# Later sums of squares in a first expert network's weight split and in the values' split, one high half a step, and sixteen squares on another engine

## The chip, the cores and the metric

The kernel runs on one core of one Trainium2 chip. The metric is the device time of one execution in microseconds, the median of several runs. Five engines of the core take part: TensorE (PE; its weight loads are PEld), VectorE (DVE), ScalarE (ACT), GpSimd (POOL) and SyncE (SP, which here only issues DMAs). Each engine takes its instructions in the order in which the program wrote them, and waits at the first whose inputs aren't ready.

## What is computed

```python
def _attn_ref(q, k, v, s):            # 4 batches, 8 heads, 576 positions, 64 wide
    scores = scale * np.matmul(q, k.transpose(0, 1, 3, 2))
    cum = np.cumsum(np.maximum(s, 0.0), axis=-1)
    bias = -(cum[:, :, :, None] - cum[:, :, None, :])
    scores = np.where(causal, -1000000000.0, scores + np.minimum(bias, 0.0))
    attn = np.exp(scores - np.max(scores, axis=-1, keepdims=True))
    return np.matmul(attn / (np.sum(attn, axis=-1, keepdims=True) + 1e-09), v)

def _moe_ref(x, w_in, w_out):         # 2304 tokens, 512 -> 2048 -> 512
    h = np.maximum(x @ w_in, 0.0)
    return h * h @ w_out

def _moe2_ref(x, w_in, w_out):
    h = x @ w_in
    return h * np.cos(h) @ w_out

x = attention output as (2304, 512); x = _moe_ref(x, ...); return _moe2_ref(x, ...)
```

## The kernel before, in words

Every matrix product is made of three products of half-precision or reduced parts (high by high, high by low, low by high; `PASSES`). A float32 operand is split for that: a high part is rounded on ScalarE, a low part is the difference, on VectorE.

The tokens go through attention and the first network in nine blocks of 256 (blocks 0 to 8). While attention works on block k + 1, the first network works on block k; block 8 has no attention beside it. Its hidden layer has 16 chunks of 128. For chunk f, `g1` (L1149) makes 12 products of 256 columns into one half of the PSUM tile `hps` (the halves alternate, L1161), `gact` (L1172) rectifies (L1177), squares (L1180) and rounds the high part `gh` (L1181), all on ScalarE, `grest` (L1184) makes the low part `gl` on VectorE (L1187), and `g2` (L1190), two chunks behind, makes 12 products into the output's PSUM.

The program is written step by step (`step`, L1326). A step holds one or two of these first and second products, a row of attention jobs, and the side work that falls due in it. Within a step each engine's queue gets, in this order: the exponentials, the first network's product, the weights' bit work and low halves (`w_step`, `w_lows`), then `gact`, then the weights' conversion of the first network (`c_step`), the scores, a second product, the transposes of attention's output (`turn`, which write the left part of the PSUM tile `xps`), the values' sums, the value products, and last `c_total`, and the values' late work.

Three pieces of side work are touched:

- The first network's first weights are used as float32 parts in blocks 0 to 2 and as float16 parts from block 3 (`KC`) on. `c_step` (L890) makes the latter in blocks 1 to 3: sixteen squares with row sums (`c_square`, L860, ScalarE), one sum over the partitions for the first `SQ_A` of them and one for the rest (`c_total`, L921, a small product into columns of `xps`), the scales from it (`c_scales`, L842, VectorE), and for each of 16 chunks an addition (`c_add`, L872, VectorE), a high half (`c_high`, L878, ScalarE) and a low half (`c_low`, L883, VectorE). The counter t is the chunk that comes next, counted from block 0.
- The values of attention are split in sixteen groups of two heads. A group has a load (`v_load`, L437, by GpSimd, into one buffer), a square with row sums (L447, ScalarE), a sum over the partitions (L453, TensorE, into `xps`), a scale (L462, VectorE), a high part (L476, ScalarE), a low part (L482, VectorE) and a store. `v_steps` sets the steps from due times, `v_add` writes the list.
- In block 8, where the second network's weights and the first network's output are prepared too: their bit work (L981, L985), clipping (L975) and squares (L1060), scales (L1076 to L1081), high halves (L1008) and low halves in pairs (L1051), and the splitting of y on GpSimd (L1241, L1253).

After block 8 the second network runs in five larger blocks of tokens (L1610, L1671, L1762).

## Time and profile before

| | us |
|---|---|
| median of 3 runs | 972.58 |
| lowest and highest | 971.02, 973.68 |
| the profiled execution | 972.91 |
| its span, first to last instruction | 970.8 |
| TensorE busy in it | 937.3 |
| VectorE, ScalarE busy | 769.7, 709.7 |

A row of a timeline gives start, duration, engine, line, operation, what is written and read, and in brackets how long the engine had been idle before it and what ended that. Several instructions of one kind stand in one row as x2 or x12. The durations of products overlap, as their ends are modelled; their starts are read. A wait that is put down to one instruction can be for several, of which that came last.

### The profile page before, as it was taken

Reading aid. Unit: us, or ns where it says so; the run is one execution under the profiler, and the core shown is the slowest. Engines: PE = TensorE matmul, PEld = TensorE weight load, DVE = VectorE, ACT = ScalarE, POOL = GpSimd, SP = SyncE. Lnnn points to the kernel's source line nnn. Section 1 sums busy time; section 2 is a strip of 40 time slices with the busy share of each in tenths; the row PEclk is TensorE's granted clock in tenths of the full one; section 3 lists DMA queues with packets and bytes.
Section 4 is the critical chain, followed back from the end, with each engine's and each line's share of the span. In section 5 each row is a group of like instructions: output and inputs, shape, how many; then the busy total and the mean of one; then the engine's idle time right before and its main releaser. Section 6 shows DMA issues by size and latency. Waiting matters only on the chain.

```text
span 970.8 us, 21039 instructions
## 1 busy us (share of the span) xinstructions
PE 937.3 (97%) x7474; PEld 726.9 (75%) x7474; DVE 769.7 (79%) x1944; ACT 709.7 (73%) x1625; POOL 159.9 (16%) x298
## 2 busy tenths in 40 slices
PE   6999999989999999999999999999999999999997
PEld 5899998988989988999989986445544456666664
DVE  6899986789798866787997375888788788798774
ACT  6799887878898767676776686677777666565553
POOL 2001123222211222222330022430000000001101
PEclk9999999999999999999999999999999999999999
DMA  8984799657998987589999679210000000112001
GB/s 246 312 271 149 168 213 227 168 145 151 200 183 191 204 195 170 134 177 174 211 215 158 217 267 362 66 44 23 1 1 1 22 1 22 49 60 67 23 22 66
DMA packets 158074, 135.38 MB, mean 139 GB/s; under 512 B 109272, under 2 KB 132128, under 8 KB 157968
## 3 DMA queue, kind: packets, MB, share of 16 engines
q1 hardware_dynamic: 147664, 123.78, 50.8%
q0 software_dynamic: 10304, 10.24, 5.2%
q8 instruction: 59, 0.97, 0.4%
q14 instruction: 47, 0.39, 0.1%
HBM read 93.91 MB, written 15.83 MB: 113 GB/s over the span
## 4 chain that ended last, share of the span: by engine, by line
PE 59%; DVE 6%; ACT 3%; issue 2%; DMA 2%; SPq 0%; DVEq 0%; ACTq 0%
PE o L1671 18%; PE hp L1610 12%; PE y L1197 11%; PE hps L1165 9%; PE bank L1762 5%; PE qkp L567 2%; PE pvs L697 2%; DVE k L415 1%; DVE sb L585 1%; DMA raw<-in_qk_dram 1%; DMA rw<-in_w_dram 1%; DMA vb<-v_d 1%; DVE wt L1678 1%; PE xps L752 0%; ACT sb L608 0%
## 5 line engine op out<-in xcount | busy, mean ns | idle before, releaser
L1197 PE MATMUL y<-gh,wt 128*128 128x256 f32 x1152 | 237.7, 289 | 0.0
L1197 PEld LDWEIGHTS y<-gh,wt 128*128 128x128 f32 x1152 | 188.6, 190 | 1.2
L1671 PE MATMUL o<-wt,gh 128*128 128x512 f16 x576 | 171.3, 379 | 1.5 <-ACT gh L1649 1.3
L1197 PE MATMUL y<-gl,wt 128*128 128x256 f32 x576 | 162.9, 283 | 0.5 <-DVE gl L1187 0.5
L1165 PE MATMUL hps<-xh,w 128*128 128x256 f16 x1152 | 142.0, 273 | 2.6 <-ACT g L1177 2.4
L1610 PE MATMUL hp<-yh,wt 128*128 128x512 f16 (+1 forms) x448 | 124.9, 348 | 0.0
L1165 PEld LDWEIGHTS <-w 128*128 128x128 f16 x1152 | 106.1, 98 | 17.8 <-issue 4.2
L1197 PEld LDWEIGHTS y<-gl,wt 128*128 128x128 f32 x576 | 109.9, 191 | 1.4 <-DVE gl L1187 0.9
L1671 PE MATMUL o<-wt,gl 128*128 128x512 f16 x288 | 109.2, 379 | 0.0
L1610 PEld LDWEIGHTS <-wt 128*128 128x128 f16 x672 | 63.9, 98 | 59.1
L1671 PEld LDWEIGHTS <-gh 128*128 128x128 f16 x576 | 56.3, 98 | 56.3 <-ACT gh L1649 1.6
L608 ACT ACTIVATE sb<-sb 128x128 f32<-128x128 f32 (+7 forms) x152 | 87.4, 575 | 4.9 <-DVE sb L585 4.3
L1177 ACT ACTIVATE g<-hps,sc 128x256 f32<-128x256 f32 x96 | 45.1, 470 | 61.3 <-PE hps L1165 59.8
L397 POOL DMA_DIRECT2D k<-ext_d x80 | 41.1, 514 | 260.2 <-PE qkp L567 159.3
L1165 PE MATMUL hps<-xh,wt 128*128 128x256 f32 x384 | 81.4, 294 | 0.3 <-ACT g L1179 0.2
L1187 DVE TENSOR_TENSOR gl<-g,gh 128x256 fp32r<-128x256 f32 x144 | 61.3, 426 | 22.8 <-ACT gh L1181 14.7
L1610 PE MATMUL hp<-yl,wt 128*128 128x512 f16 (+1 forms) x224 | 78.0, 348 | 0.0
L585 DVE CUSTOM_DVE_ANT_0 sb<-qkp,mask 128x128 f32<-128x128 f32 (+7 forms) x152 | 69.3, 456 | 5.3 <-PE qkp L552 4.3
L656 DVE SCALAR_TENSOR_TENSOR p<-sb,p 128x384 f16<-128x384 f32 (+3 forms) x120 | 66.3, 553 | 8.8 <-ACT p L650 5.6
L1635 ACT ACTIVATE a<-kf 128x512 f32<-128x512 f32 (+1 forms) x80 | 46.5, 583 | 31.4 <-DVE kf L1630 30.4
L405 ACT CAST hi<-raw 128x704 fp32r<-128x704 f32 (+2 forms) x80 | 58.8, 735 | 13.6 <-DMA raw<-in_qk_dram 7.2
L1165 PEld LDWEIGHTS hps<-xh,wt 128*128 128x128 f32 x384 | 64.5, 195 | 2.8 <-issue 1.2
(172 smaller groups left out, 2006.8 us busy)
## 6 DMA issues: line engine op xcount, KB each, us to landing
rw<-in_w_dram SPq DMA_DIRECT2D x64, 512.0 KB
raw<-in_qk_dram SPq DMA_DIRECT2D x48, 352.0 KB
yr<-y_d SPq DMA_DIRECT2D x17, 512.0 KB
raw<-in_qk_dram SPq DMA_DIRECT2D x16, 384.0 KB
v_d<-vt SPq DMA_DIRECT2D x16, 320.0 KB
vb<-v_d SPq DMA_DIRECT2D x32, 160.0 KB
vr<-in_v_dram POOLq DMA_DIRECT2D x15, 320.0 KB, 5.4
y_d<-yst SPq DMA_DIRECT2D x18, 256.0 KB
```

The costliest lines, as they stand in the source:

```text
L405: nc.scalar.copy(hi[:, BT - nq:BT + nk], raw[:, BT - nq:BT + nk])
L585: nc.vector.tensor_tensor_reduce(out=sb[0:r, c0:c0 + cn], in0=p[0:r, 0:cn], in1=mask[0:r, mo:mo + cn], scale=-0.125, scalar=(3.0e38 if k = ...
L608: nc.scalar.activation(out=sb[0:r, 0:w], in_=sb[0:r, 0:w], func=ACTF.Exp, scale=-1.0, bias=j["nb"], accum_out=z[0:r, ti, x:x + 1],)
L656: nc.vector.scalar_tensor_tensor(out=p[0:r, cw:cw + w], in0=sb[0:r, 0:w], scalar=PSC, in1=p[0:r, 0:w], op0=ALU.mult, op1=ALU.subtract,)
L1165: nc.tensor.matmul(hp, w[:, a, c * 128:(c + 1) * 128], (xh, xl)[e][:, c, :], start=(n == 0), stop=(n == 3 * KD - 1),)
L1177: nc.scalar.activation(out=g, in_=hp, func=ACTF.Relu, scale=hs1[:, f // 2:f // 2 + 1])
L1187: nc.vector.tensor_tensor(out=gl, in0=g, in1=gh, op=ALU.subtract)
L1197: nc.tensor.matmul(yps[k][d // 2][:, d % 2, :], w[:, a, d * 128:(d + 1) * 128], (gh, gl)[e], start=(f == 0 and n == 0 and d % 2 == 0), sto ...
L1610: nc.tensor.matmul(hp, chunk_of(w, a, c), (yh, yl)[e][:, c, :], start=(m == 0), stop=(m == 3 * KD - 1),)
L1635: nc.scalar.activation(out=a, in_=kf, func=ACTF.Sin, scale=-6.2831850)
L1671: nc.tensor.matmul(ops[j][a], (gh, gl)[e][:, a * 128:(a + 1) * 128], w[:, x, :], start=(first and m == 0), stop=(last and m == 2),)
L1762: nc.tensor.matmul(bank[b][:, 0:HB], w[:, a, wx, c * 128:(c + 1) * 128], y_side(j, yx, e, c), start=(start and n == 0), stop=(n == 5), ski ...
```

## The change

The constants: `SQ_A` goes from 12 to 10, so that the first sum covers ten squares and the second six; `CONV_PACE` from 1.7 to 1.5 chunks between additions; `V_TIME` from 7 to 8, which starts each group of values a step earlier. In `v_add` a group's sum, scale, parts and store come a step later after its square. In `c_step` a high half is made only when none was made earlier in the same step, and one addition a step instead of as many as are due; the last squares come one a chunk instead of one in two chunks. `c_total` sends its sums only when the counter has passed a limit some chunks after the last square, instead of in that square's step. In `gact`, block 8's square is no ScalarE square of the rectified product any more: a VectorE instruction multiplies the product in PSUM by its scale and by the rectified value.

```diff
--- before.py
+++ after.py
@@ -38,8 +38,8 @@
 G2LAG = 2
 PASSES = ((0, 0), (0, 1), (1, 0))
 KC = 3
-CONV_PACE = 1.7
-SQ_A = 12
+CONV_PACE = 1.5
+SQ_A = 10
 
 
 def _weave(*chains):
@@ -126,7 +126,7 @@
 TURN_FROM = 24
 V_STRIDE = 11
 V_NEAR = 6
-V_TIME = 7
+V_TIME = 8
 
 
 @with_exitstack
@@ -529,9 +529,9 @@
             if g not in vs:
                 fs, t = [(t, v_load)], t + 2
             late = g == gs[2]
-            fs += [(t + 2, v_wait)] * late
-            fs += [(t, v_square), (t + 1 + late, v_sum), (t + 2, v_scale), (t + 2, v_high), (t + 3, v_low)]
-            for x, f in fs + [(t + 3, v_store)] * stored:
+            fs += [(t + 3, v_wait)] * late
+            fs += [(t, v_square), (t + 2 + late, v_sum), (t + 3, v_scale), (t + 3, v_high), (t + 4, v_low)]
+            for x, f in fs + [(t + 4, v_store)] * stored:
                 vq.extend([] for _ in range(x + 1 - len(vq)))
                 vq[x].append((f, g))
 
@@ -893,7 +893,7 @@
         for c in clow:
             c_low(c)
         clow.clear()
-        while chigh and (chigh[0][1] + 2 <= t or last is not None and chigh[0][0] <= last):
+        while chigh and (not clow and chigh[0][1] + 2 <= t or last is not None and chigh[0][0] <= last):
             c, _ = chigh.pop(0)
             while clow:
                 c_low(clow.pop(0))
@@ -906,23 +906,23 @@
         c_scales()
         n = 0
         while cdone[0] < NF and n < 1 and t >= (
-            NF + 2 + cdone[0] if cdone[0] < SQ_A else 2 * NF + 2 + 2 * (cdone[0] - SQ_A)
+            NF + 2 + cdone[0] if cdone[0] < SQ_A else 2 * NF + 2 + (cdone[0] - SQ_A)
         ):
             c_square(cdone[0])
             cdone[0] += 1
             n += 1
-        while cdone[1] < cdone[2] and t >= (KC - 1) * NF + 1 + int(cdone[1] * CONV_PACE) and (
+        if cdone[1] < cdone[2] and t >= (KC - 1) * NF + 1 + int(cdone[1] * CONV_PACE) and (
             cdone[1] not in (1, 2) or cdone[1] - 1 in w16 and cdone[1] - 1 not in w32
         ):
             c_add(cdone[1])
             chigh.append((cdone[1], t))
             cdone[1] += 1
 
-    def c_total():
-        if cdone[0] == SQ_A and SQ_A not in csent:
+    def c_total(t):
+        if cdone[0] == SQ_A and SQ_A not in csent and t > NF + SQ_A + 4:
             csent.append(SQ_A)
             c_sums(0, SQ_A)
-        elif cdone[0] == NF and NF not in csent:
+        elif cdone[0] == NF and NF not in csent and t > 2 * NF + (NF - SQ_A) + 4:
             csent.append(NF)
             c_sums(SQ_A, NF)
 
@@ -1177,7 +1177,12 @@
             nc.scalar.activation(out=g, in_=hp, func=ACTF.Relu, scale=hs1[:, f // 2:f // 2 + 1])
         else:
             nc.scalar.activation(out=g, in_=hp, func=ACTF.Relu)
-        nc.scalar.activation(out=g, in_=g, func=ACTF.Square)
+        if k == NB1 - 1:
+            nc.vector.scalar_tensor_tensor(
+                out=g, in0=hp, scalar=hs1[:, f // 2:f // 2 + 1], in1=g, op0=ALU.mult, op1=ALU.mult
+            )
+        else:
+            nc.scalar.activation(out=g, in_=g, func=ACTF.Square)
         nc.scalar.copy(gh, g)
         gd[k, f] = (g, gh)
 
@@ -1391,8 +1396,8 @@
                 emit_pv(j)
         if attn and behind:
             values(i)
-        if moe:
-            c_total()
+        if moe and slots:
+            c_total(slots[0][1])
         p_turn()
         w_ahead()
         if attn:
```

## Rows read from the trace of the kernel before

**Rows 1.** The page: busy time of the engines, share of the span, instructions

```profile
PE 937.3 (97%) x7474; PEld 726.9 (75%) x7474; DVE 769.7 (79%) x1944; ACT 709.7 (73%) x1625; POOL 159.9 (16%) x298
```

**Rows 2.** Busy time by stretch: length, then engines, granted clock, DMA share, GB/s

```profile
200.00:220.00 20.00, 17.23 (x156) 16.15 (x156) 17.61 (x70) 16.24 (x46) 3.93 (x10) 1.00 0.51 127
560.00:580.00 20.00, 18.17 (x161) 16.84 (x160) 13.58 (x27) 17.08 (x40) 5.18 (x5) 1.00 0.87 305
...
620.00:640.00 20.00, 20.00 (x97) 9.06 (x95) 18.04 (x30) 14.62 (x28) 7.29 (x6) 1.00 0.16 52
```

**Rows 3.** TensorE's waits: us in total, times, longest; the last from 540 to 600

```profile
PE pvs L697 <- DVE xp L737: 2.2, 3, 1.3
...
PE xps L836 <- ACT wj L862: 1.3, 1, 1.3
...
PE xps L752 <- DVE yss L849: 0.8, 1, 0.8
...
PE hps L1165 <- ACT g L1177: 2.2, 3, 1.3
```

**Rows 4.** Timeline at the first sum: start, duration, what, idle time before it

```profile
172.52 0.15 DVE L462 TENSOR_SCALAR vsc<-xps 128x2 int32<-128x2 int32 x1
...
172.79 0.16 DVE L849 TENSOR_SCALAR yss<-xps 128x12 f32<-128x12 f32 x1
...
173.01 0.27 PE L752 MATMUL xps<-ident,xp 64*128 64x64 f32 x1 [0.82 <-DVE yss L849]
```

**Rows 5.** Timeline at the second sum

```profile
205.76 1.33 ACT L878 ACTIVATE w<-w,sc 128x512 f16<-128x512 f32 x2
...
207.00 0.61 ACT L862 ACTIVATE wj<-wt 128x512 bf16<-128x512 f32 x1
...
207.76 0.16 PE L836 MATMUL xps<-yss,ones 128*128 128x4 bf16 x1 [1.26 <-ACT wj L862]
```

**Rows 6.** Timeline, block 8: chunk 0's rectifier and chunk 1's first product

```profile
545.94 0.46 ACT L1177 ACTIVATE g<-hps,sc 128x256 f32<-128x256 f32 x1
...
546.45 1.47 PE L1165 MATMUL hps<-xh,w 128*128 128x256 f16 x12
```

**Rows 7.** Timeline, block 8: low halves in chunk 7's step, chunk 8's first product

```profile
565.51 1.41 DVE L1051 SCALAR_TENSOR_TENSOR wt<-st,wsc,wt 128x512 f16<-128x512 f32 x2
...
566.23 1.47 PE L1165 MATMUL hps<-xh,w 128*128 128x256 f16 x12
```

**Rows 8.** Timeline, block 8: the same at chunks 10 and 12

```profile
575.13 1.42 DVE L1051 SCALAR_TENSOR_TENSOR wt<-st,wsc,wt 128x512 f16<-128x512 f32 x2 [0.47 <-ACT wt L1008]
...
575.62 0.45 ACT L1177 ACTIVATE g<-hps,sc 128x256 f32<-128x256 f32 x1
...
576.12 1.47 PE L1165 MATMUL hps<-xh,w 128*128 128x256 f16 x12 [1.30 <-ACT g L1177]
...
582.31 1.41 DVE L1051 SCALAR_TENSOR_TENSOR wt<-st,wsc,wt 128x512 f16<-128x512 f32 x2
...
582.79 1.47 PE L1165 MATMUL hps<-xh,w 128*128 128x256 f16 x12 [0.33 <-ACT g L1177]
```

**Rows 9.** Timeline, block 8: low halves in chunk 15's step, chunk 15's low part

```profile
591.99 1.41 DVE L1051 SCALAR_TENSOR_TENSOR wt<-st,wsc,wt 128x512 f16<-128x512 f32 x2
...
593.33 0.43 DVE L1187 TENSOR_TENSOR gl<-g,gh 128x256 fp32r<-128x256 f32 x1
```

**Rows 10.** Line 1180 (ns min/median/max), and a group of line 1641 (us, mean ns)

```profile
L1180 ACT ACTIVATE g<-g x144: 416/418/422, 45.3 to 592.4; 128x256 f32<-128x256 f32 x144
...
L1641 DVE SCALAR_TENSOR_TENSOR a<-hp,gsc,a 128x256 f32<-128x256 f32 x16 | 7.7, 481 | 1.8 <-ACT a L1635 1.8
```

**Rows 11.** Timeline, block 8: a scale on VectorE beside GpSimd

```profile
573.20 1.12 POOL L1241 TENSOR_SCALAR yr<-yr,ysc 128x1024 f32<-128x1024 f32 x1
573.27 1.07 DVE L1081 TENSOR_SCALAR wsc<-wex 128x2 int32<-128x2 int32 x1
```

**Rows 12.** GpSimd's waits for VectorE's split of values: us in total, times, longest

```profile
POOL vr L437 <- DVE vt L482: 4.2, 2, 2.8
```

## The prediction

> **What bounds the kernel now.** I read the engine shares first: TensorE is busy for 97% of the span and no other engine comes near [rows 1]. Its work can't shrink, because the change touches no product of any size, so the question is only which of TensorE's few waits go and which come. The table by stretches then says where there are any: from 620 to 640 us TensorE has none, from 560 to 580 it idles 1.83 us, and from 200 to 220 it idles 2.77 us [rows 2]. The list of TensorE's waits names them: in the first network the sums of squares (1.3 us on ScalarE and 0.8 us behind the reading of those sums) and a value product that waits for VectorE (2.2 us), in the last block of that network the first product (2.2 us in three waits for the rectifier) [rows 3]. All that is later is a stage in which TensorE runs without a gap, so a microsecond won or lost before 595 us should reach the end nearly whole.
>
> **Sums of the weights' squares.** Before, the first sum (12 columns) leaves TensorE at the end of the step in which the twelfth square is made. The next step holds only a second product, and VectorE reaches the sums late: it takes the values' scale at 172.52 and the sums at 172.79, and the transposes, which write other columns of the same PSUM tile, start at 173.01 after 0.82 us of waiting [rows 4]. After, the sum has 10 columns and goes out one step later, and VectorE reads it in a step with a first and a second product. The values' scale stays where it was, ending 0.28 us before the sums' reading ends (172.67 against 172.95), so I count 0.3 us won. The second sum is the dearer one: in that step ScalarE makes two high halves (1.33 us) and then the last square, and the sum, which is queued in TensorE behind nothing else, waits 1.26 us for it [rows 5]. After, the step holds one high half, and the sum follows five steps later: 1.26 us won. Its reading by VectorE then lies in a step with two products again, so I expect no new wait there. Taking one high half out of that step also spares VectorE a low half in it; the value product's wait of up to 1.3 us soon after [rows 3] may shrink, but TensorE also comes to it earlier. I count 0.2 us. Together 1.7 us; for the low end 0.5 us, if the stretch turns out to be held by ScalarE and VectorE and only a part of the 1.26 us is kept, for the high end 3.0 us, if the 1.3 us go as well.
>
> **Squares and high halves moved.** Two of the sixteen squares move from block 1 to block 2, one of them into a step with a high half; high halves come one to a step, and additions one to a step. No instruction is added. The words of the change say that steps with two heads make no squares; the diff has nothing of the kind, only this limit on high halves, and a step can still hold a high half and a square. I count nothing: products of the second kind are two chunks behind the rectifier, which covers a ScalarE instruction or two. Uncovered, each square would cost about what the last one did, up to 1.3 us [rows 5].
>
> **Sums of the values' squares.** The groups start one step earlier (0, 6, 12, ... instead of 0, 7, 13, ...) and their sum comes two steps after the square instead of one, so except for the first group sum, scale and store stay in the steps they had. No TensorE wait of before names these squares, so nothing is won. The loads are moved by one step, into the step that splits the group before. They are issued by GpSimd into the one buffer that VectorE's split reads, and so wait for that split at the head of GpSimd's queue; behind them stand the loads of the heads' bias rows and the clearing of padding. Before, two of them waited so, 2.8 us at most [rows 12]. A head's rows are loaded two heads ahead, which covers that; I count zero, with 1.5 us either way as bounds from the same row and from the one wait of 1.3 us above.
>
> **The last block's squares.** This is the large term. Sixteen ScalarE squares of 0.42 us go and sixteen VectorE instructions come that multiply a PSUM product by a scale and by the rectified value. The same form with the same shape stands in the last network at 481 ns [rows 10]. ScalarE wins nothing by it: its queue holds rectifier, square, copy back to back, and in place of the square the copy now waits for VectorE, 0.48 us and two handovers of about 0.05 us. What matters is who else waits. Two chunks' first products share one PSUM tile, and the product of the next chunk starts 0.05 us after the rectifier has read this one: rectifier until 546.40, product at 546.45 [rows 6]. After, it must wait for the new reader too, and that stands in VectorE's queue behind all the step's other work.
>
> In four of the sixteen steps this work ends in a pair of low halves of the second network's weights. Chunk 7: the pair ends at 565.51 + 1.41 = 566.92; with 0.03 to start, 0.48 and 0.05 the next product can start at 567.48 instead of 566.23 [rows 7], 1.25 us late. Chunks 10 and 12 in the same way: 577.11 instead of 576.12, and 584.28 instead of 582.79, 0.99 and 1.49 us [rows 8]. Chunk 15 has no next product, but its copy would end at 594.37 and its low part at 594.83 instead of 593.76 [rows 9], and the last products wait for that: 1.07 us. Together 4.80 us. In five steps without a pair (0, 8, 9, 11, 13) the product follows the rectifier as closely as in chunk 0, each worth up to 0.53 us, in chunk 2 half of that: at most 2.9 us more.
>
> These don't simply add. A late chunk makes ScalarE late as well, and the next tight step is then late on both sides. The 1.30 us that TensorE already waits before chunk 11 [rows 8] can absorb part of what came before it. If all of it does, 4.80 - 1.30 = 3.5 us is the low end. The high end is 4.80 + 2.9 = 7.7 us. Walking the sixteen steps with these durations, each engine in its order, I find +0.5 us after chunk 0 and +0.5 after chunk 2 (ScalarE is still late from chunk 0 and the slack of 0.28 us there is used up), nothing in 3 to 6, where TensorE itself is last, +1.2 after 7, +0.8 after 8 and 9 together, +0.2 after 10 and 11, whose waits of before absorb nearly all, +1.2 after 12, +0.1 after 13 and 14, and +0.6 at the end, where the 0.5 us that the last second products waited before is used up. That is 5.1 us, which I take.
>
> One cost is not in that walk: VectorE's instructions beside GpSimd's. A scale of two columns took 1.07 us, ending with GpSimd's instruction of 573.20 [rows 11]. If the new instruction were held in the same way in the three steps in which GpSimd splits y, 0.6 us each, it would add 1.8 us, which is inside the high end. The Trainium skill (GPSIMD Engine Reference, Specifications) says that the two engines contend where VectorE runs a two-port mode or reads two SBUF operands; the new instruction reads one operand from PSUM, so by that rule it isn't held and the sum stays. No row here shows the 256 column form beside GpSimd's splitting.
>
> **The sum.** Against the profiled execution, 972.91 us (its span of 970.8 and 2.1 us around it): -1.7 + 5.1 = +3.4, 976.3 us. That execution is 0.33 us above the median of the three runs, so I forecast 976.0 us. The case's own range is 972.6 + 3.5 - 3.0 = 973.1 to 972.6 + 7.7 - 0.5 = 979.8.
>
> **The rivals.** First, faster: the next product is not held by the new instruction, because what holds it follows columns and not the tile. Then only the path through copy and low part is left, with two chunks of cover, and the last pair's 1.07 us at most. It takes the first part's 1.7 to 3.0 us: 972.6 + 1.07 - 1.7 = 972.0, or 969.6 where the tail is covered too and the high end is won. It decides from where less than 1.7 us of the 4.80 is paid. Against it stands that seven of the fifteen products there start just 0.05 us after the other half's rectifier, in chunk 0 and again in chunk 10, where it ends at 576.07 [rows 6, 8]. The Trainium skill (PSUM — Partial Sum Buffer, on bank collisions) speaks against this change too: it asks for semaphores by bank and quadrant, not by address. By that rule the forecast stands, since both halves lie in one bank; the rows agree with 0.05 us. Second, the stretch before 300 us gives more: value products and transposes stop waiting for VectorE, 1.5 us beyond the high end's 3.0. Then 972.6 + 5.1 - 4.5 = 973.2. For it speaks that the two 1.3 us waits are VectorE's and ScalarE's queues, against it that most VectorE work there only changes steps. Third, slower still: a moved square and a GpSimd load that waits for a split each open a wait of 1.3 to 1.5 us in a stretch where the first part should win. Then -1.7 becomes about +1.1, and 972.6 + 5.1 + 1.1 = 978.8.
>
> **How the numbers follow.** The forecast gets 0.60, the first rival 0.16, the second 0.12, the third 0.12. A measurement here can tell about 0.3% from no change, 2.9 us: faster is below 969.7, slower above 975.5. Of the forecast about three quarters lie above 975.5 (0.43), the rest within; of the third rival nearly all are slower (0.11). Of the first rival and the second 0.11 are faster, the rest within. So slower 0.54, same 0.35, faster 0.11. The range that leaves out no more than 2 in 10 runs from 971.5, inside the first rival, to 979.0, inside the high end of the forecast.
>
> **What would show it.** In the profile after: no wait of TensorE on line 862's square, and a transposes' wait at the values' scale of half a microsecond; in block 8 the three waits of the first product now end with VectorE's new line, longest after chunks 7, 10 and 12, and the block lasts some 5 us longer, while GpSimd's waits at the value loads grow and TensorE's don't. I am wrong if the product of chunk 8 starts before the new instruction of chunk 7 has ended, if VectorE takes the new instruction ahead of the low halves, or if the stage after it turns out to have slack that swallows what block 8 lost.

## The result, and the profile after

The changed kernel takes 986.51 us in the median (981.58 to 988.16) against 972.23 us before (971.02 to 973.68). The ratio, worked out over all runs, is 1.0138, 95% interval 1.0097 to 1.0179. It is slower, as forecast, but by 14.3 us in the medians (13.4 by the ratio) and not by 3.4, and so beyond 979.0 us, where the range ended. The profiled execution took 988.16 us, its span 986.3 us against 970.8 before.

Where the time went is read from two products that both kernels have. The first product of block 8 starts at 543.50 us before and at 553.81 after, 10.3 us later; the first product of the second network (L1610 before, L1615 after) at 595.22 and at 611.88, 16.7 us later. Before and after in turn:

```profile
543.50 0.28 PE L1165 MATMUL hps<-xh,w 128*128 128x256 f16 x1
553.81 0.28 PE L1165 MATMUL hps<-xh,w 128*128 128x256 f16 x1
...
595.22 0.39 PE L1610 MATMUL hp<-yh,wt 128*128 128x512 f16 x1
611.88 0.39 PE L1615 MATMUL hp<-yh,wt 128*128 128x512 f16 x1
```

From there to TensorE's last product the distance stays; what follows that product is 1.2 us shorter after. So 10.3 us are lost ahead of block 8, where the sum had a gain of 1.7, and 6.4 us in block 8, where it had a loss of 5.1. Each trace is one execution: the kernel with block 8's squares alone, whose program ahead of block 8 is that of before, starts the block at 541.09 us. So a distance ahead of block 8 is good to some 2.4 us only.

TensorE's waits after (us in total, times, longest), to be held against [rows 3]:

```profile
PE hps L1165 <- DVE g L1181: 6.3, 7, 2.3
...
PE pvs L697 <- DVE xp L737: 3.3, 3, 1.8
PE qkp L567 <- DVE z L733: 2.8, 1, 2.8
PE qkp L567 <- DVE k L415: 2.7, 1, 2.7
...
PE xps L836 <- DVE vsc L462: 0.5, 1, 0.5
...
PE xps L836 <- DVE xh L825: 0.3, 1, 0.3
```

The first row is block 8, as expected: the first product now waits for VectorE's new line. The wait for line 862's square [rows 5] is gone: that second sum (L836) now waits 0.3 us, for VectorE's L825. The 0.5 us is the first sum's own wait, at the values' scale. What the sum had at nothing are the two waits of 2.8 and 2.7 us at L567, the scores' products with the heads' rows `k`. Here is GpSimd's queue ahead of the first of them, and the product (a timeline; in brackets the idle time before it and what ended that):

```profile
156.79 0.74 POOL L437 DMA_DIRECT2D vr<-in_v_dram  x1 [6.48 <-DVE vt L482]
157.53 0.51 POOL L397 DMA_DIRECT2D k<-ext_d  x1
158.03 0.54 POOL L398 DMA_DIRECT2D k<-in_qk_dram  x1
...
158.70 0.52 POOL L397 DMA_DIRECT2D k<-ext_d  x1
159.21 0.55 POOL L398 DMA_DIRECT2D k<-in_qk_dram  x1
...
162.36 0.61 PE L567 MATMUL qkp<-k 68*128 68x320 f32 x1 [2.76 <-DVE z L733]
```

GpSimd stood 6.48 us at the value load, because the load's one buffer was still read by VectorE's split (L482); before, the longest such wait was 2.8 us [rows 12]. Behind it two heads' rows were late, and their loads went out back to back. The trace gives 4.2 us from issue to landing for the one of 158.03: it lands at 162.2, and the product starts at 162.36. The releaser in the brackets is only the instruction that ended last near by; the load is the one that fits. The second wait is alike: by the trace's semaphores the rows issued at 339.16, behind a value load, land at 344.89, and the product starts at 345.03, in both cases 0.14 us after the landing.

During or after such a wait TensorE's granted clock fell. The columns are the stretch, its length, the busy time of PE, PEld, DVE, ACT, POOL, then the granted clock (1.00 is 2.4 GHz, 0.50 is 1.2 GHz), DMA share and GB/s:

```profile
160.00:162.00 2.00, 0.00 (x0) 0.00 (x0) 1.79 (x7) 1.77 (x5) 0.00 (x0) 0.80 1.32 207
162.00:164.00 2.00, 1.64 (x7) 1.68 (x8) 0.31 (x3) 0.91 (x3) 0.32 (x1) 0.50 1.10 278
164.00:166.00 2.00, 2.00 (x14) 1.91 (x13) 0.00 (x0) 0.78 (x1) 0.94 (x3) 0.50 0.87 307
166.00:168.00 2.00, 2.00 (x19) 2.00 (x17) 1.31 (x3) 0.00 (x0) 0.00 (x0) 0.50 0.01 1
...
344.00:346.00 2.00, 0.97 (x6) 0.83 (x7) 1.48 (x4) 0.00 (x0) 0.05 (x1) 0.88 0.78 201
346.00:348.00 2.00, 2.00 (x11) 1.42 (x10) 0.49 (x2) 0.00 (x0) 0.99 (x2) 0.50 0.29 81
348.00:350.00 2.00, 2.00 (x22) 1.96 (x20) 0.00 (x0) 1.66 (x4) 0.00 (x0) 0.77 0.05 4
...
598.00:600.00 2.00, 2.00 (x11) 1.44 (x11) 0.42 (x1) 2.00 (x5) 0.00 (x0) 0.52 0.97 354
600.00:602.00 2.00, 2.00 (x13) 1.94 (x12) 0.48 (x1) 0.89 (x4) 0.00 (x0) 0.62 1.02 412
```

TensorE idled through 160 to 162, and from 162.36 to 168 it ran at 0.50: about 2.8 us of work at full clock were not done in those 5.6 us. Before, the clock also fell here, but for a shorter time, in the same rows of the kernel before:

```profile
160.00:162.00 2.00, 2.00 (x22) 1.91 (x22) 1.13 (x4) 0.91 (x3) 1.25 (x3) 0.65 1.11 236
162.00:164.00 2.00, 2.00 (x13) 2.00 (x11) 1.73 (x4) 0.00 (x0) 0.00 (x0) 0.50 1.00 338
164.00:166.00 2.00, 2.00 (x19) 2.00 (x18) 0.18 (x2) 0.83 (x2) 0.60 (x2) 1.00 0.80 155
```

The falls at 346 and 598 are new. Each of the three goes with a TensorE wait of over 2 us (one that ends at 162.36, 345.03 and 597.99); no term of the sum was for this.

### The profile page after: what moved, and what is told of

It reads as the page before. It is cut to its first block, busy times and chain, and to the rows that moved or that the text cites. A ratio compares the mean times of both kernels' runs of the same rounds, so it can differ in the third digit from the quotient of the medians.

```text
span 986.3 us, 21033 instructions
## 1 busy us (share of the span) xinstructions
PE 942.1 (96%) x7474; PEld 730.9 (74%) x7474; DVE 775.7 (79%) x1961; ACT 702.8 (71%) x1608; POOL 159.6 (16%) x298
## 4 chain that ended last, share of the span: by engine, by line
PE 55%; DVE 8%; issue 3%; ACT 3%; DMA 1%; POOL 0%; DVEq 0%; ACTq 0%; POOLq 0%; SPq 0%
PE o L1676 17%; PE hp L1615 12%; PE y L1202 8%; PE hps L1165 8%; PE bank L1767 5%; PE qkp L567 2%; PE pvs L697 2%; DVE k L415 1%; DVE sb L585 1%; DMA k<-in_qk_dram 1%; DVE gl L1192 1%; DVE g L1181 1%; ACT g L1177 1%; DVE st L985 1%; DVE wt L1683 0%
## 5 line engine op out<-in xcount | busy, mean ns | idle before, releaser
L1165 PE MATMUL hps<-xh,w 128*128 128x256 f16 x1152 | 144.4, 276 | 7.5 <-DVE g L1181 6.3
L1615 PE MATMUL hp<-yh,wt 128*128 128x512 f16 (+1 forms) x448 | 124.9, 348 | 0.0
L1615 PEld LDWEIGHTS <-wt 128*128 128x128 f16 x672 | 64.0, 98 | 59.0
L1177 ACT ACTIVATE g<-hps,sc 128x256 f32<-128x256 f32 x96 | 45.2, 471 | 66.6 <-PE hps L1165 63.5
L1615 PE MATMUL hp<-yl,wt 128*128 128x512 f16 (+1 forms) x224 | 78.0, 348 | 0.0
L1186 ACT CAST gh<-g 128x256 fp32r<-128x256 f32 x144 | 58.5, 406 | 16.4 <-DVE g L1181 12.4
```

The lines of the kernel that those rows point to most:

```text
L1165: nc.tensor.matmul(hp, w[:, a, c * 128:(c + 1) * 128], (xh, xl)[e][:, c, :], start=(n == 0), stop=(n == 3 * KD - 1),)
L1177: nc.scalar.activation(out=g, in_=hp, func=ACTF.Relu, scale=hs1[:, f // 2:f // 2 + 1])
L1186: nc.scalar.copy(gh, g)
L1615: nc.tensor.matmul(hp, chunk_of(w, a, c), (yh, yl)[e][:, c, :], start=(m == 0), stop=(m == 3 * KD - 1),)
```

## The experiments

First each part alone, then the two parts that lose, taken apart, then a version that is faster than both. A ratio, to the kernel before, is worked out over all runs and stands with its 95% interval; the quotient of the two medians differs from it by up to 0.0016. 0.001 is 0.97 us. A trace is of one execution of its run. A diff is against the kernel before, unless the sentence ahead of it names another.

### The parts alone

**The values' part.**

```diff
-V_TIME = 7
+V_TIME = 8
-fs += [(t, v_square), (t + 1 + late, v_sum), (t + 2, v_scale), ...
+fs += [(t, v_square), (t + 2 + late, v_sum), (t + 3, v_scale), ...
```

> The kernel before with the values' part of the change alone (V_TIME 8, sum two steps after the square). Theory A (GpSimd's queue): a value load now stands in the step of the split that frees its buffer, waits at the head of GpSimd's queue for it, and the bias rows behind it land late; TensorE then waits about 2.7 us at a score product and the granted clock falls to half for a few microseconds: 5 to 10 us slower than before, with the first score waits of over 2 us somewhere between 150 and 360 us, and block 8 as before. Theory B (the moved weights' squares and additions crowd ScalarE and VectorE): within 1 us of before.

Measured: 1.0112 (1.0085 to 1.0139), 11 us. Its trace has the waits at L567 of the whole change, and falls of the clock after them:

```profile
PE qkp L567 <- DVE k L415: 2.9, 1, 2.9
...
PE qkp L567 <- DVE z L733: 2.8, 1, 2.8
```

The part that was counted at nothing carries most of the loss.

**The weights' part** (`CONV_PACE`, `SQ_A`, the conditions in `c_step` and `c_total`).

```diff
-CONV_PACE = 1.7
-SQ_A = 12
+CONV_PACE = 1.5
+SQ_A = 10
-        elif cdone[0] == NF and NF not in csent:
+        elif cdone[0] == NF and NF not in csent and t > 2 * NF + (NF - SQ_A) + 4:
```

> The kernel before with the weights' part alone (SQ_A 10, CONV_PACE 1.5, one high half and one addition a step, later sums). Theory A: 0 to 2 us faster than before, the wait on line 862's square gone, no score wait over 1.5 us that wasn't there before. Theory B: 5 to 10 us slower, with the wait of about 1 us for the rectifier near 128 us and the later ones.

Measured: 0.9995 (0.9977 to 1.0014), which doesn't tell 1.7 us from nothing. The trace shows what was won, and what was lost elsewhere (the two sums, then waits of the value products):

```profile
170.47 0.17 PE L836 MATMUL xps<-yss,ones 128*128 128x10 bf16 x1 [0.54 <-DVE vsc L462]
...
217.66 0.17 PE L836 MATMUL xps<-yss,ones 128*128 128x6 bf16 x1 [0.25 <-DVE xh L825]
...
PE pvs L697 <- DVE xp L737: 2.0, 2, 1.8
PE pvs L697 <- DMA vb<-v_d: 1.9, 2, 1.3
```

The second sum's wait fell from 1.26 us to 0.25. At the first one the transposes' wait of 0.82 us [rows 4] is gone, and the sum itself waits 0.54 at the values' scale, so 0.28 are won. The value products' waits for VectorE fell only from 2.2 to 2.0 us in all, with a longer one among them (1.8 us at 212.82), and those for their values' loads, at 376 to 379 us, rose from 0.8 to 1.9. That last loss is not steady: the run with the weights' part and the second tile, below, has one wait of 0.4 us for such a load.

**Block 8's squares.**

```diff
-        nc.scalar.activation(out=g, in_=g, func=ACTF.Square)
+        if k == NB1 - 1:
+            nc.vector.scalar_tensor_tensor(out=g, in0=hp, scalar=hs1[...], in1=g, op0=ALU.mult, op1=ALU.mult)
+        else:
+            nc.scalar.activation(out=g, in_=g, func=ACTF.Square)
```

> The kernel before with block 8's squares on VectorE alone. By the prediction's walk 5.1 us slower than before; by the profile of the changed kernel 6.3 us, all of it between 543 us and the start of the second network, of which 1.7 us are a fall of the granted clock near the end of block 8 if TensorE waits there over 2 us. Rival: in the changed kernel block 8 was hurt by what arrived late from before it; then alone it costs 3 us or less.

Measured: 1.0044 (1.0026 to 1.0062), 4.3 us. In its trace block 8 lasts from 541.09 to 598.17 us, 57.1 against 51.7 before: 5.4 us. The place of the largest wait, chunk 12's step:

```profile
581.02 1.06 DVE L1081 TENSOR_SCALAR wsc<-wex 128x2 int32<-128x2 int32 x1
...
583.36 0.45 ACT L1177 ACTIVATE g<-hps,sc 128x256 f32<-128x256 f32 x1
...
583.38 1.41 DVE L1051 SCALAR_TENSOR_TENSOR wt<-st,wsc,wt 128x512 f16<-128x512 f32 x2
584.71 0.48 DVE L1181 SCALAR_TENSOR_TENSOR g<-hps,sc,g 128x256 f32<-128x256 f32 x1
...
585.24 0.27 PE L1165 MATMUL hps<-xh,w 128*128 128x256 f16 x1 [2.27 <-DVE g L1181]
```

The rectifier ends at 583.81, the pair of low halves at 584.79, the new instruction at 585.19, and the product starts 0.05 us later: VectorE's queue stands between, as the prediction had it. This wait of 2.27 us brought no fall of the clock: the mean granted clock of the run is 1.000.

**All but the values' part**: the kernel after, with these lines as before.

```diff
-V_TIME = 8
+V_TIME = 7
-fs += [(t, v_square), (t + 2 + late, v_sum), (t + 3, v_scale), ...
+fs += [(t, v_square), (t + 1 + late, v_sum), (t + 2, v_scale), ...
```

> The changed kernel with the values' part undone. Theory A: the weights' and the square's parts add up, 4 to 6.5 us slower than before, and 8 to 10 us faster than the changed kernel. Theory B: nearly as slow as the changed kernel, 12 us or more above before.

Measured: 1.0050 (1.0035 to 1.0065). With it the values' part is worth 0.9% within the whole, and 1.1% alone.

### The values' part taken apart

**The load's place alone.**

```diff
-                fs, t = [(t, v_load)], t + 2
+                fs, t = [(max(0, t - 1), v_load)], t + 2
```

> The kernel before with one thing moved: each value load one step earlier, so that most stand in the step that splits the group before, as in the changed kernel; squares, sums, scales and splits stay where they were. Theory A (the load waits at the head of GpSimd's queue and holds the bias rows behind it): 5 to 11 us slower than before, with one or two score waits of over 2 us. Rival (the squares a step earlier and the sums a step later after them cost the time): within 1.5 us of before.

Measured: 1.0076 (1.0049 to 1.0103). The waits name the cause:

```profile
PE qkp L567 <- DMA k<-in_qk_dram: 10.4, 5, 3.2
```

**The values' part with the load left where it was**: the values' part alone, and on it

```diff
-                fs, t = [(t, v_load)], t + 2
+                fs, t = [(t + (t > 0), v_load)], t + 2
```

> The values' part of the change alone, but with each load after the first one step later, so that it comes a step after the split that frees its buffer and one step before its square instead of two. Theory A: most of the 11 us come back, 0 to 4 us slower than before (a load takes about 5 us to land and a step about 4, so ScalarE may now wait for it), and no score wait over 2 us. Rival: still 8 us or more slower.

Measured: 1.0050 (1.0032 to 1.0068), 4.9 us, more than theory A's 4. No product waits for a head's rows by more than the kernel before has, but nearly half of the loss stays. It has another name: waits for the rectifier, 5.9 us in six at L1177 against 2.4 in four before, and 1.5 in three at L1179 against 0.2 in one. Four of the six lie in block 8, three of them as before. The other two, 1.45 and 1.81 us, and two at L1179, 0.96 and 0.39, stand behind a values' square on ScalarE. The row, and then the longest of them:

```profile
PE hps L1165 <- ACT g L1177: 5.9, 6, 1.8
```

And the timeline there:

```profile
382.57 0.74 ACT L447 ACTIVATE vt<-vr 128x640 f16<-128x640 f32 x1 [4.62 <-DMA v_d<-vt]
383.22 0.19 ACT L447 ACTIVATION_READ_ACCUMULATOR vt<-vr 128x1 f32 x1
383.31 0.19 ACT L808 COPY x<-xps 128x64 f32<-128x64 f32 x1
383.40 0.48 ACT L1177 ACTIVATE g<-hps,sc 128x256 f32<-128x256 f32 x1
...
383.93 0.27 PE L1165 MATMUL hps<-xh,w 128*128 128x256 f16 x1 [1.81 <-ACT g L1177]
```

The values' square, moved a step earlier and itself waiting for its buffer's last store, stands right ahead of the rectifier on ScalarE. What ScalarE waited for ahead of these squares (us in total, times), first before, then in this run:

```profile
  DMA v_d<-vt: 1.4, 2
...
  DMA v_d<-vt: 12.0, 5
  DMA vr<-in_v_dram: 1.8, 2
```

The square writes into the buffer `vt`, from which the store of the group ahead still reads; before, it came a step later. So the part loses twice, and in the same way: an instruction moved towards what frees its buffer waits at the head of a queue. The load costs 7 us (the run ahead of this one), the rest 5, together about the 11 us measured. That the rest is the square's is read from the waits; no run moves the square alone.

**The early load from another queue.** The five waits could still be the early transfer's own cost. Here the same load goes out in the same early step, issued by SyncE: on the kernel with the load's place alone

```diff
-        eng = nc.sync if g[:2] == (V_ORDER[0], 0) else nc.gpsimd
+        eng = nc.sync
```

> The kernel before with the values' loads one step earlier, as in the run that measured 1.0076, but issued by SyncE instead of GpSimd; nothing else is changed. In that run TensorE waited five times, 10.4 us in all, for loads of a head's rows that GpSimd issues. Theory A: these waits come from GpSimd's queue alone, because the value load waits there for a split and the heads' rows stand behind it; then TensorE's waits for these rows shrink to under 3 us here, and the ratio falls to 1.000 to 1.004 if what stands behind the load in SyncE's queue has slack, or stays above that with TensorE's waits under another name (the value products' or the scores' operands that SyncE loads) if it has none. Theory B: the early load itself costs (its transfer beside the others, or the buffer's turn); then the waits for the heads' rows stay at 8 us or more and the ratio at 1.006 to 1.009, whichever engine issues it.

Measured: 0.9968 (0.9953 to 0.9983), 968.46 us against 971.07. No wait for a head's rows is left in the trace; the only ones at L567 of any size are those that the kernel before has, too:

```profile
PE qkp L567 <- DVE sb L585: 2.3, 6, 0.6
...
PE qkp L567 <- DVE k L415: 0.4, 1, 0.4
```

That settles it: not the early load, but what stands behind it in GpSimd's queue. SyncE's queue isn't empty either, but the load adds little waiting there: the store of the group ahead, which waits for the same split, stands before it. A split that ends at 153.20 us lets out the store (153.22) and the load right behind it (153.65); 12 of the 16 loads follow such a store within 1 us. The Trainium skill (DMA: Bandwidth & Descriptors, Issuing engines are not separate DMA queues) says that issuing from several engines saves only the time that a sequencer needs to issue. By that the time should hardly differ, and here it does: the issuing queue alone made 1.0076 or 0.9968, because a queue is also an order of waiting.

**The whole values' part from SyncE**: the values' part alone, and on it

```diff
-        eng = nc.sync if g[:2] == (V_ORDER[0], 0) else nc.gpsimd
+        eng = nc.sync
```

> The whole values' part alone, which measured 1.0112, with its loads issued by SyncE instead of GpSimd. Theory A (two separate costs: GpSimd's queue behind the early load, and the squares that now stand ahead of the rectifier): only the first goes, 1.004 to 1.007, with TensorE's waits for the rectifier at over 4 us as in the run with the later load. Theory B (the early load costs wherever it is issued): 1.009 to 1.013.

Measured: 1.0039 (1.0025 to 1.0053): two thirds of the loss gone, the square's part left. The waits for the rectifier (L1177 and L1179) came to 4.4 us, as expected, but before has 2.6 of them, so not all of the rest is named by them; 2.0 us stand at the values' scale (L462), where before has 0.9. This trace can't name the whole rest: its execution, 971.09 us, is the shortest of the five, and the others took 974.66 to 975.57.

**The whole change from SyncE**: the kernel after, and on it

```diff
-        eng = nc.sync if g[:2] == (V_ORDER[0], 0) else nc.gpsimd
+        eng = nc.sync
```

> The whole change, with the values' loads issued by SyncE instead of GpSimd; nothing else differs from the kernel after, which measured 1.0138. In the values' part alone this step took the ratio from 1.0112 to 1.0039, by 0.0073. Theory A (GpSimd's queue is the larger half of the loss, and the parts add): 1.005 to 1.008, what the moved squares of the values (0.0039) and block 8's squares (0.0044) leave, less 0.0005 for the weights' part; no wait of TensorE for a head's rows over 1 us. Theory B (the whole change loses more than its parts, through the falls of the clock): 1.009 to 1.012.

Measured: 1.0094 (1.0074 to 1.0113), in theory B's range, with an interval that reaches into theory A's. That the whole loses more than its parts isn't shown by it: the parts, 3.8 - 0.5 + 4.3 = 7.6 us, lie within the measured 7.2 to 11.0. In the trace the queue's part is back: block 8's first product starts 1.4 us later than before (544.95) instead of 10.3, and no wait for a head's rows is over 0.4 us. What is left, 7.6 us at the second network, is block 8's 6.1 and these 1.4. The ratios give back less (0.0044) than in the part alone (0.0073), with intervals of 0.001 to 0.004 on either side. The trace is of the shortest of the four executions (979.13 us, the others 981.53 to 982.96), and the clock falls in it three times, at 214, 238 and 590 us; what the rest of the difference is stays open.

### Block 8's squares taken apart

The prediction held the next first product responsible, which must wait for the new reader of the shared PSUM tile. The next three runs take away what it waits for, in part or whole.

**The squares ahead of the low halves** (in block 8 the pairs are queued behind the step's square): block 8's squares alone, and on it

```diff
-        w_lows()
+        if not last8[0]:
+            w_lows()
...
         act(n)
+        if last8[0]:
+            w_lows()
```

> Block 8's squares on VectorE alone (as in the run of that part alone), but in block 8 the step's pair of low halves is queued on VectorE behind the rectifier and the new instruction instead of ahead of them. If the pairs ahead cost the time, the four waits of together 4.8 us shrink and the loss of about 4 to 5 us falls to 0.5 to 2 us. If the handover itself costs it (0.5 us in each tight step), 3 us or more remain.

Measured: 1.0020 (1.0003 to 1.0038), some 2 us less than the squares alone, though the two intervals overlap. In the trace block 8 lasts only 0.7 us less (4.7 us over before), with as many waits for the new line (5.7 us in seven).

**A PSUM tile of its own for the odd chunks**: block 8's squares alone, and on it

```diff
-        hp = hps[:, f % 2, :]
+        hp = hps[:, f % 2, :] if k < NB1 - 1 or f % 2 == 0 else hps2[0][:, f % 2, :]
```

> Block 8's squares on VectorE alone, with the odd chunks' first products of block 8 in a PSUM tile of their own, so that a product no longer waits for the reader of the chunk before it. If what counts is the product held by the new instruction, 3 us or more of the loss come back, and only the last copy's 1 us stays. If ScalarE's wait in front of the copy counts, the loss stays at 3 us or more.

Measured: 1.0045 (1.0023 to 1.0066): nothing is won. The first products do come free, though. At chunk 12's they are 1.8 us ahead of the kernel before, counted from the beginning of the block, and then the last steps, among them a wait of 2.7 us for a low part with a fall of the clock behind it, take back more than that. This trace is of the longest of the ten executions (979.65 us, median 976.20).

**Both together**: block 8's squares alone, and on it

```diff
-        hp = hps[:, f % 2, :]
+        hp = hps[:, f % 2, :] if k < NB1 - 1 or f % 2 == 0 else hps2[0][:, f % 2, :]
...
+        if last8[0]:
+            w_lows()
```

> Part four alone (block 8's squares on VectorE), with both of the earlier remedies at once: the first products of odd chunks in a PSUM tile of their own, and the low halves of the second network's weights queued behind the step's squares. Alone, the second tile left the whole loss of 4.3 us (1.0045) and the other order left half of it (1.002). Theory A: the loss is the first product's wait for the square and the squares' wait for the pairs of low halves, and the second tile alone failed only because the last chunks' low part then stood behind the last steps' scales and pair; with both the ratio is 0.999 to 1.001. Theory B: what remains is ScalarE's own wait inside a chunk (rectifier, then 0.55 us of waiting, then the copy) and the scales ahead of the low part in the last two steps, which neither remedy moves; then 1.002 to 1.004, with a wait of TensorE of over 1 us for a low part near the end of block 8.

Measured: 1.0028 (1.0014 to 1.0041), which is theory B's. The timeline at the end of block 8:

```profile
588.65 2.30 POOL L1259 TENSOR_TENSOR yl<-yr,yh 128x512 f16<-128x512 f32 x2 [6.87 <-ACT yh L1258]
...
589.50 0.49 DVE L1182 SCALAR_TENSOR_TENSOR g<-hps,sc,g 128x256 f32<-128x256 f32 x1 [0.99 <-ACT g L1178]
...
590.09 0.89 DVE L1077 TENSOR_SCALAR wex<-wsm 128x2 int32<-128x2 int32 x1
...
590.92 1.13 POOL L1247 TENSOR_SCALAR yr<-yr,ysc 128x1024 f32<-128x1024 f32 x1
591.01 1.06 DVE L1081 TENSOR_SCALAR wsc<-wex 128x2 int32<-128x2 int32 x1
...
593.05 0.42 DVE L1193 TENSOR_TENSOR gl<-g,gh 128x256 fp32r<-128x256 f32 x1
...
593.53 0.38 PE L1203 MATMUL y<-gl,wt 128*128 128x256 f32 x1 [2.67 <-DVE gl L1193]
```

The last scales stand ahead of the low part on VectorE, two of them stretched to 0.89 and 1.06 us beside GpSimd, and the second product waits 2.67 us for that low part. So the shared tile decides only where the lateness is paid, at a first product or at a second one. The timeline points to the length of VectorE's and ScalarE's queues in the last four steps, where the change adds 0.48 us a chunk; no run shortens these queues, so that is argued and not shown. These four steps lose 6.5 us in this trace, 1.7 of them in a fall of the clock behind that wait; the twelve ahead of them win 2.4.

**The second tile without the change.**

```diff
-        hp = hps[:, f % 2, :]
+        hp = hps[:, f % 2, :] if k < NB1 - 1 or f % 2 == 0 else hps2[0][:, f % 2, :]
```

> The kernel before with one thing changed: in block 8 the first products of odd chunks go into a PSUM tile of their own, so that a product needn't wait for the rectifier of the chunk ahead. In the trace of before these waits are 1.30, 0.53 and 0.33 us. If the shared tile is what makes them, up to 2.2 us come back, 0.9978 to 0.9995. If the wait is for the rectifier of two chunks ahead, or if the same time is lost one step later at the second product, 0.9995 to 1.0005.

Measured: 0.9996 (0.9980 to 1.0011). The kernel before shows the same: its three waits of the first product go, and this one comes, against 0.5 us before. The first twelve chunks win 2.4 us here as well, and the last four give back 2.2.

```profile
PE y L1198 <- DVE gl L1188: 2.8, 2, 2.2
```

**The change with all mendings**: the kernel after, with both edits of block 8 as above, and

```diff
-                fs, t = [(t, v_load)], t + 2
+                fs, t = [(t + (t > 0), v_load)], t + 2
```

> The whole change with the three mendings: the values' loads one step later (in the step after the split of the group ahead), the low halves of the second network's weights queued behind the squares in block 8, and the second PSUM tile there. The whole change measured 1.0138. If the parts add, the values' part leaves 1.005 and the weights' part -0.0005; the squares leave what the run with both remedies leaves (0 to 0.004 by the two theories). So 1.004 to 1.006 if the squares' loss is healed, 1.006 to 1.009 if not. If the parts don't add (one part's lateness lands in another's slack), it is outside these.

Measured: 1.0063 (1.0045 to 1.0082). The parts add (0.0050 - 0.0005 + 0.0028 = 0.0073, within the interval). That block 8's loss isn't healed is read from the trace, in which the block still lasts 55.7 us against 51.7; the interval alone covers both forecasts.

### Towards a faster version

**The weights' part and the second tile**: the weights' part alone, and on it

```diff
-        hp = hps[:, f % 2, :]
+        hp = hps[:, f % 2, :] if k < NB1 - 1 or f % 2 == 0 else hps2[0][:, f % 2, :]
```

> Part one and two alone (the sums of the weights' squares later, one high half a step), with the second PSUM tile of block 8. As a candidate to beat the kernel before: if the first part's 1.6 us in the trace are real but small against the spread (0.9995 measured), and the second tile gives up to 2 us, 0.996 to 0.998; if what the weights' part wins before 300 us is given back whole, and block 8 is bound by other waits, 0.9990 to 1.0005.

Measured: 0.9979 (0.9964 to 0.9994): faster than before, by 2.0 us by the ratio and 1.3 in the medians (969.77 against 971.10).

**SyncE at the steps of before.**

```diff
-        eng = nc.sync if g[:2] == (V_ORDER[0], 0) else nc.gpsimd
+        eng = nc.sync
```

> The kernel before with the values' loads issued by SyncE instead of GpSimd, in the steps where they were. With the load one step earlier as well the ratio was 0.9968. If that gain comes from taking the loads out of GpSimd's queue, where two of them already waited for a split (2.8 us at most), it is here too, 0.996 to 0.998; if it needs the earlier step (values that are there earlier), 0.999 to 1.001.

Measured: 0.9987 (0.9975 to 0.9999), between the two: taking the loads out of GpSimd's queue gives some of the 0.9968, the earlier step probably the rest, though the two intervals overlap.

**All that was free or better**: the weights' part and the second tile, and on them

```diff
-        eng = nc.sync if g[:2] == (V_ORDER[0], 0) else nc.gpsimd
+        eng = nc.sync
-                fs, t = [(t, v_load)], t + 2
+                fs, t = [(max(0, t - 1), v_load)], t + 2
```

> What the runs showed to be free or better, together: the kernel before with the values' loads one step earlier and issued by SyncE (0.9968), the weights' part of the change (0.9995), and the second PSUM tile in block 8 (0.9996; weights and second tile together 0.9979). If these add, 0.994 to 0.996; if they win the same slack, 0.9955 to 0.998.

Measured: 0.9972 (0.9958 to 0.9985). It beats both kernels, but isn't shown to beat the early load from SyncE by itself (0.9968): the gains don't add.

## Why the prediction was right and wrong

**The values' part is the step that failed.** It said "A head's rows are loaded two heads ahead, which covers that; I count zero". Alone, the part measured 10.9 us. The cover was not worked out: GpSimd waited 6.5 and 8.4 us for the split instead of up to 2.8, and behind the first of these stood not one head's rows but two. The rows showed that the load waits for the split, and the prediction named what is queued behind it; what it lacked was the slack of those rows, the time from their issue to the product that reads them. The bound of 1.5 us came from a wait of before [rows 12], in a queue in which the load had one step more. The third rival had this mechanism and one more square, at "1.3 to 1.5 us" each; the runs give some 7 us for the load and 5 for the rest. Both come in several steps, not in one: with the load alone moved there are five waits for rows, and without it four for a rectifier behind a values' square.

**That nothing is won where "no TensorE wait of before names these squares"** was right, but it was used to leave out a loss as well. A square in another step is ahead of another rectifier, and nearer to the store that frees its buffer: ScalarE's waits ahead of these squares grew from 1.4 us to 11.6 in the changed kernel (13.8 with the load left where it was).

**The clock was in no term.** Three falls lie in the changed kernel's trace, each with a wait of over 2 us, against one before. The rows from 160 to 168 give 3.4 us of missing clock (0.4 in the first, in which TensorE idled, 1.0 in each of the three others) against 1.7 before; the falls at 346 and 598 give 1.7 each. Ahead of block 8 the two waits (5.5 us) and the clock (3.0 more than before) make up 8.5 of the 10.3 us in the trace. A fall makes a wait dearer than its length, though not each wait brings one.

**Block 8's squares: the mechanism and the size were right for this kernel.** The walk against the trace of the squares alone, in us, read from the first products' starts:

| chunks | walk | trace |
|---|---|---|
| 0 | 0.5 | 0.5 |
| 1 to 6 | 0.5 | 0.5 |
| 7 | 1.2 | 1.1 |
| 8, 9 | 0.8 | 0.6 |
| 10, 11 | 0.2 | 0.2 |
| 12 | 1.2 | 2.0 |
| 13 to the end | 0.7 | 0.5 |
| sum | 5.1 | 5.4 |

The ratio says 4.3 us (2.5 to 6.0). Chunk 12 was undersized: the scale that its pair of low halves needs (L1081) now stands behind chunk 11's new instruction on VectorE. It began 0.35 us after chunk 12's first product before (579.92 against 579.57) and 0.95 us after it here (581.02 against 580.07), and the pair came 0.6 us later with it. Of this, 0.26 us are the scale ahead of it (L1077), which took 0.87 us there instead of 0.61, both beside GpSimd. The first rival's condition was wrong, as the product waits for the new instruction (0.05 us after it, at 585.24). Where a second tile makes the condition true, the time is lost all the same, since the path through copy and low part has no two chunks of cover in the last steps.

**The new instruction beside GpSimd** is not held: it takes 0.49 us at 589.50 in the rows above, within GpSimd's 588.65 to 590.95, where the neighbouring scale took 0.89. The trace of after has three more such places, 0.47 to 0.49 us at 584.43, 592.27 and 604.46. That agrees with the Trainium skill (GPSIMD Engine Reference, Specifications), which names contention for VectorE instructions in a 2-port mode or with two SBUF inputs, as the prediction used it.

**The weights' part** was -1.7 and measured -0.5 us (-2.2 to +1.4), so its size is not settled. In its trace the terms came nearly as forecast: 0.28 us at the first sum (forecast 0.3), 1.0 at the second (1.26, as 0.25 us of waiting stays), and the value products' 0.2. Against them stand 1.1 us more of waiting for the values' loads, which no term had.

**The sum of the parts** as measured, -0.5 + 10.9 + 4.3 = 14.7 us, agrees with the 13.4 us (9.4 to 17.4) of the whole. Slack in the second network swallowed nothing, as the prediction had it: its products keep the 16.7 us to TensorE's last one.

## What to carry to other kernels

A DMA whose buffer is still read waits at the head of the queue that issues it, here for up to 8.4 us: before it is moved to such a step, look up what is queued behind it, and how long that has from issue to use; or issue it from a queue that waits for the same thing already. The same goes for an instruction that writes into a buffer which a store still reads. A shared buffer that shows up as the wait need not be the bound: give it a second one, and see whether the wait goes or moves. Of work that is put in another step, ask which critical instruction of that step now stands behind it, even where the trace of before names no wait for it.

## What the hardware showed

- The granted clock fell from 2.4 to 1.2 GHz with waits of TensorE of over 2 us, but not with each: 2.29 us in block 8 of the changed kernel was followed by a fall, 2.27 us at the same place with the squares alone left it at 1.000. It fell after a shorter wait too: in the values' part with the load left where it was, at 207.8 us behind one of 1.47 us. In the kernel before it is at 0.50 from 162 to 164 us, with TensorE busy for all of the 2 us ahead of that.
- VectorE's integer scales of two columns take 0.17 us alone and, in block 8 before and after, 0.55 to 1.08 beside GpSimd, and stand in the path that ends block 8; the new instruction, with an operand from PSUM, keeps its 0.48 us there.
